# Loading x and the gate weights in the queue of the big transfers

## Chip, cores, metric

The kernel runs on one core of one Trainium2 chip. The metric is the device time of one execution in microseconds (us); lower is better. When a time is given without further words it is a median of several runs.

## The reference, cut to what matters

One token per batch row (B = 2), D = 1024. The model mixes an attention block over a long cache with an MLP block, by a gate.

```python
g = sigmoid((x * gate_w).sum(-1, keepdims=True))        # x: (2, 1, 1024), gate_w: (1024,)
# attention: 32 heads, head size 128, 16384 cached positions, bf16
q = (x @ wq)                                            # wq: (1024, 4096)
p = softmax(einsum("bhqd,bhkd->bhqk", q, k_cache) * 128**-0.5)
a = einsum("bhqk,bhkd->bhqd", p, v_cache)  ... @ wo
b = ...                                                 # layernorm, w1, gelu, w2, layernorm, w3, gelu, w4
return g * a + (1 - g) * b
```

Nearly all the work is reading the K and V caches: 2 x 2 x 32 x 16384 x 128 bf16 values, 537 MB out of the 573 MB that the kernel reads.

## The kernel before

The caches come in 32 steps. A step i needs a K tile and a V tile of 8.39 MB each (two heads of one batch row, 64 KB in each of 128 partitions). Three buffers of that size form a ring (`NBIG = 3`), and wq, which is just as large, goes through the same ring. A transfer is issued, always on SyncE (SP), once the buffer it takes is free: the order is wq, K0, K1 (three buffers, at once), then V0 (takes wq's buffer), K2 (takes K0's), V1 (takes K1's), K3 (takes V0's), and so on.

```python
    def load_rows(keys, srcs):                       # wq, and the MLP weights later
        t = big_tile("wt")
        ...
            nc.sync.dma_start(out=v, in_=src.rearrange("(p r) n -> p r n", p=P))

    x_pm = const.tile([P, B, KC], BF16)              # KC = 8
    gw_pm = const.tile([P, KC], BF16)
    with nc.allow_non_contiguous_dma(reason="a few KB"):
        nc.scalar.dma_start(out=x_pm[:], in_=A_x.rearrange("b s (p r) -> p (b s) r", p=P))
        nc.scalar.dma_start(out=gw_pm[:], in_=gate_w.rearrange("(p r) -> p r", p=P))
    ...                                              # constants
    xT = const.tile([P, KC, B], BF16)
    nc.vector.tensor_copy(out=xT[:], in_=x_pm[:].rearrange("p b r -> p r b"))

    def compute_gate():
        nc.vector.tensor_tensor(out=prod[:], in0=x_pm[:], in1=gw_pm[:]..., op=ALU.mult)
        nc.vector.reduce_sum(out=part[:], in_=prod[:], axis=AX.X)
        ...

    def compute_q():
        wq = wt.pop("wq")
        for h in range(H):
            for r in range(KC):
                nc.tensor.matmul(qps[:, h, :], lhsT=wq[:, r, h * Dh : (h + 1) * Dh], rhs=xT[:, r, :], ...)
        nc.vector.tensor_copy(out=qT[:], in_=qps[:])
        ...                                          # 8 small matmuls, qsel

    def qk_stage(i):                                 # 32 transposes and 64 matmuls on K tile i
        ...
                nc.vector.transpose(out=T[:], in_=Kw[:, m * CJ : (m + 1) * CJ, wh, :])
    ...
    xfers = [("big", "q", lambda: load_rows(["wq"], [A_wq]))]
    steps = [("q", compute_q), ("gate", compute_gate)]
    for i in range(-1, NT):                          # then k{i+1}, v{i}, wo rows, softmax, ...
    ...
    def issue_ready():                               # issue a load when the step that frees its buffer is recorded
```

x_pm takes 16 bytes from each of 2 batch rows for each of 128 partitions: 256 pieces of 16 bytes. gw_pm takes 128 such pieces. A scheduler fixes the order of the instructions on each engine when the program is built. On VectorE it puts `prod` (which needs gw_pm) ahead of `qT`.

## Time and profile before

| | before |
|---|---|
| time, median | 1369.87 us (1369.75 to 1370.2, 3 runs) |
| span of the profiled run | 1367.8 us |
| bytes moved, mean rate | 573.46 MB, 419 GB/s |
| rate from 400 to 800 us | 431 GB/s, DMA share 1.00 |
| rate from 70 to 130 us | 298 GB/s |

The page of the kernel before: its span, the rate in 40 equal slices of 34 us, and the DMA queues (packets, MB, share of 16 engines). q1 is the queue of SP, q10 that of ScalarE (ACT).

```profile
span 1367.8 us, 14339 instructions
...
GB/s 422 434 280 336 428 426 430 434 426 438 426 436 434 434 425 434 428 432 436 435 430 432 434 432 430 432 428 432 430 434 427 431 428 429 432 426 434 431 414 230
...
q1 hardware_dynamic: 15392, 572.53, 97.4%
...
q10 hardware_dynamic: 416, 0.01, 0.0%
```

The stream runs at 414 to 438 GB/s in every slice except the third, the fourth and the last. As the bytes alone take 573.46 / 0.431 = 1330 us at the steady rate, only time in which the DMA engines stand still can be won.

The windows view of the same kernel, by stretch (us from the start): length, then busy time and count for TensorE, its weight load, VectorE, ScalarE and GpSimd, then TensorE's granted clock, the DMA share and GB/s.

```profile
70.00:80.00 10.00, 8.51 (x29) 2.71 (x28) 9.20 (x15) 0.00 (x0) 0.00 (x0) 1.00 0.97 419
80.00:90.00 10.00, 8.34 (x29) 2.60 (x27) 8.76 (x14) 0.00 (x0) 0.00 (x0) 1.00 0.00 1
90.00:100.00 10.00, 5.36 (x18) 2.25 (x18) 7.36 (x16) 0.78 (x2) 0.33 (x1) 0.83 1.03 419
...
110.00:120.00 10.00, 8.97 (x60) 3.51 (x62) 7.63 (x12) 0.00 (x0) 0.34 (x1) 1.00 0.29 105
```

Twice the stream stops (a packet is counted where it starts): from 80 to 90 us, and for some 7 us between 110 and 120 us. VectorE is busy for 88% of the first of these stretches: the core computes, and the DMA engines wait. The timeline of SP (start, length, the issue) shows for what: the next load is issued only when a buffer is free.

```profile
0.74 0.36 SPq L119 DMA_DIRECT2D wt<-in_A_wq_dram  x1
1.16 0.89 SPq L97 DMA_DIRECT2D Kn<-in_A_k_cache_dram  x2
52.20 0.33 SPq L108 DMA_DIRECT2D Vn<-in_A_v_cache_dram  x1
89.54 0.33 SPq L97 DMA_DIRECT2D Kn<-in_A_k_cache_dram  x1
117.49 0.33 SPq L108 DMA_DIRECT2D Vn<-in_A_v_cache_dram  x1
```

K2 is issued at 89.54 us, when K0 has been worked through, and V1 at 117.49 us, when K1 has. Both come after the stream has run dry. The work on K0 itself begins late. From the DMA view (source, queue, size, us from issue to landing) and the timeline of VectorE and TensorE; the bracket is the idle time before, and what ended it:

```profile
x_pm<-in_A_x_dram ACTq DMA_DIRECT2D x1, 4.0 KB, 41.4
wt<-in_A_wq_dram SPq DMA_DIRECT2D x1, 21.9
gw_pm<-in_gate_w_dram ACTq DMA_DIRECT2D x1, 2.0 KB, 61.7
```

```profile
42.12 0.17 DVE L195 COPY xT<-x_pm 128x16 bf16<-128x16 bf16 x1 [39.85 <-DMA x_pm<-in_A_x_dram]
42.35 6.08 PE L237 MATMUL misc<-xT,wt 128*128 128x2 bf16 x223 [42.35 <-DVE xT L195]
...
63.01 0.17 DVE L213 TENSOR_TENSOR prod<-x_pm,gw_pm 128x16 f32<-128x16 bf16 x1 [20.71 <-DMA gw_pm<-in_gate_w_dram]
...
64.36 0.22 DVE L244 CAST qT<-misc 128x64 bf16<-128x64 f32 x1
...
65.93 1.30 DVE L284 STREAM_TRANSPOSE T<-Kn 128x512 f32<-128x512 f32 x2
```

8.39 MB of wq land 21.9 us after issue; 4 KB of x take 41.4 us and 2 KB of gate weights 61.7 us. The projection waits for x until 42 us. Its result qT could be copied at 52 us, but `prod` stands ahead of it on VectorE and waits for the gate weights until 63 us. The first K transpose starts at 65.93 us, long after K0 has landed (42.3 us).

### The profile page before, as it was taken

The page shows a single profiled execution, that of the slowest core. Times are in us where ns is not written, and L with a number is a line of the kernel's source. Part 1 is how long each engine was busy: PE and PEld are TensorE (multiplying, and loading weights), DVE is VectorE, ACT ScalarE, POOL GpSimd, SP SyncE. Part 2 cuts the span into 40 slices and gives each one's busy share as a digit, 9 for nine tenths or more (in the row PEclk, how much of TensorE's full clock was granted, in tenths as well). Part 3 has the DMA queues.
Part 4 walks back from the last instruction along what each step waited for, and adds up shares of the span by engine and source line. Part 5 has one row for each costly group of instructions (what it writes and reads, how often), then busy time and mean ns, then how long its engine had stood idle before and what let it go on. Part 6 is the DMA issues. An engine that isn't in the chain of part 4 may idle for free.

```text
span 1367.8 us, 14339 instructions
## 1 busy us (share of the span) xinstructions
PE 901.4 (66%) x5707; PEld 401.5 (29%) x5770; DVE 783.3 (57%) x1373; ACT 45.0 (3%) x99; POOL 14.3 (1%) x45
## 2 busy tenths in 40 slices
PE   0277766776667766776666676667766666776667
PEld 0223322342223522322222342223222222322224
DVE  0187756755556356666555545566665555666554
ACT  0000000000000000000000000000000000000000
POOL 0000000000000000000000000000000000000000
PEclk9999988868888588888888868888888888888887
DMA  9967999999999999999999999999999999999995
GB/s 422 434 280 336 428 426 430 434 426 438 426 436 434 434 425 434 428 432 436 435 430 432 434 432 430 432 428 432 430 434 427 431 428 429 432 426 434 431 414 230
DMA packets 15876, 573.46 MB, mean 419 GB/s; under 512 B 2369, under 2 KB 2369, under 8 KB 6721
## 3 DMA queue, kind: packets, MB, share of 16 engines
q1 hardware_dynamic: 15392, 572.53, 97.4%
q8 instruction: 45, 0.74, 0.2%
q14 instruction: 23, 0.18, 0.0%
q10 hardware_dynamic: 416, 0.01, 0.0%
HBM read 572.53 MB, written 0.00 MB: 419 GB/s over the span
## 4 chain that ended last, share of the span: by engine, by line
DMA 53%; PE 26%; DVE 16%; another core or an unknown queue 2%; issue 2%; ACT 1%; SPq 0%; ACTq 0%
DMA Kn<-in_A_k_cache_dram 46%; PE S L289 19%; DVE T L284 15%; PE O L333 4%; DMA Vn<-in_A_v_cache_dram 4%; DMA x_pm<-in_A_x_dram 3%; PE misc L343 1%; PE wo_acc L379 1%; ACT Os L341 1%; PE misc L200 1%; ACT Pr L317 0%; DVE PT L321 0%; DVE OT L371 0%; DVE mx L310 0%
## 5 line engine op out<-in xcount | busy, mean ns | idle before, releaser
L284 DVE STREAM_TRANSPOSE T<-Kn 128x512 f32<-128x512 f32 x1024 | 688.3, 701 | 220.6 <-DMA Kn<-in_A_k_cache_dram 152.7
L289 PE MATMUL S<-T,z_135 128*128 128x512 bf16 x992 | 328.4, 419 | 142.9 <-DVE T L284 130.9
L289 PE MATMUL S<-T,z_137 128*128 128x512 bf16 x993 | 325.2, 414 | 144.7 <-DVE T L284 131.8
L289 PEld LDWEIGHTS <-z_135 128*128 128x128 bf16 x1024 | 107.0, 104 | 361.4 <-issue 308.1
L289 PEld LDWEIGHTS <-z_137 128*128 128x128 bf16 x1024 | 106.4, 104 | 360.1 <-issue 305.9
L333 PE MATMUL O<-Vn,PT 128*32 128x512 bf16 x1984 | 114.1, 382 | 0.0
L371 DVE TENSOR_TENSOR OT<-misc,rinv 128x2 bf16<-128x2 f32 x32 | 5.2, 162 | 152.0 <-PE misc L343 144.7
L333 PEld LDWEIGHTS <-PT 128*32 128x32 bf16 x1984 | 70.7, 140 | 43.1 <-issue 13.7
L341 ACT COPY Os<-O 128x512 f32<-128x512 f32 x31 | 18.2, 587 | 1095.4 <-PE O L333 1095.4
L343 PE MATMUL misc<-osel,Os 128*128 128x2 f32 x248 | 32.7, 254 | 12.6 <-ACT Os L341 11.2
L431 PEld LDWEIGHTS <-wt 128*128 128x128 bf16 x576 | 35.9, 169 | 16.4 <-DMA wt<-in_B_w_dram 15.1
L321 DVE STREAM_TRANSPOSE PT<-Pr 128x512 bf16<-128x512 bf16 x32 | 22.7, 711 | 28.7 <-ACT Pr L317 28.7
L237 PE MATMUL misc<-xT,wt 128*128 128x2 bf16 x256 | 7.1, 165 | 45.1 <-DVE xT L195 42.3
L343 PEld LDWEIGHTS misc<-osel,Os 128*128 128x128 f32 x248 | 30.0, 191 | 21.1 <-ACT Os L341 21.1
L300 DVE TENSOR_REDUCE m<-S 128x1 f32<-128x512 f32 x32 | 22.2, 692 | 22.5 <-PE S L289 22.5
L310 DVE TENSOR_REDUCE mx<-misc 64x1 f32<-64x64 f32 x64 | 14.2, 222 | 23.7 <-PE misc L200 23.3
L317 ACT ACTIVATE Pr<-S,nb 128x512 bf16<-128x512 f32 x32 | 22.0, 688 | 122.1 <-DVE nb L312 119.1
L379 PEld LDWEIGHTS <-woh 128*128 128x128 bf16 x256 | 20.7, 168 | 10.4 <-issue 10.2
L195 DVE COPY xT<-x_pm 128x16 bf16<-128x16 bf16 x1 | 0.2, 175 | 39.9 <-DMA x_pm<-in_A_x_dram 39.9
L379 PE MATMUL wo_acc<-OT,woh 128*128 128x2 bf16 x256 | 20.1, 200 | 4.0 <-DVE OT L371 4.0
L200 PE MATMUL misc<-mdiag,ones_f 128*128 128x128 f32 x64 | 16.5, 343 | 8.5 <-DVE mdiag L303 8.5
L237 PEld LDWEIGHTS <-wt 128*128 128x128 bf16 x256 | 7.1, 104 | 45.0 <-DMA wt<-in_A_wq_dram 22.7
(173 smaller groups left out, 160.7 us busy)
## 6 DMA issues: line engine op xcount, KB each, us to landing
wt<-in_B_w_dram SPq DMA_DIRECT2D x2, 7168.0 KB, 46.7
woh<-in_A_wo_dram SPq DMA_DIRECT2D x32, 256.0 KB, 29.9
wt<-in_B_w_dram SPq DMA_DIRECT2D x2, 2048.0 KB, 36.2
Vn<-in_A_v_cache_dram SPq DMA_DIRECT2D x1, 4096.0 KB, 39.5
Vn<-in_A_v_cache_dram SPq DMA_DIRECT2D x1, 2048.0 KB, 43.7
Vn<-in_A_v_cache_dram SPq DMA_DIRECT2D x1, 1024.0 KB, 45.6
Vn<-in_A_v_cache_dram SPq DMA_DIRECT2D x2, 512.0 KB, 47.8
Kn<-in_A_k_cache_dram SPq DMA_DIRECT2D x32, 48.8
```

What stands on the lines that cost most here:

```text
L200: nc.tensor.matmul(ps[:], lhsT=ones_f[:], rhs=src, start=True, stop=True)
L237: nc.tensor.matmul(qps[:, h, :], lhsT=wq[:, r, h * Dh : (h + 1) * Dh], rhs=xT[:, r, :], start=(r == 0), stop=(r == KC - 1),)
L284: nc.vector.transpose(out=T[:], in_=Kw[:, m * CJ : (m + 1) * CJ, wh, :])
L289: nc.tensor.matmul(S[:], lhsT=z[:, 2 * wh + par, NM - 1 - m : NM - 1 - m + P], rhs=Tb[:, :, par], start=(m == 0 and wh == 0 and par == 0), ...
L300: nc.vector.reduce_max(out=m[:], in_=S[:], axis=AX.X)
L317: nc.scalar.activation(out=Pr[:], in_=S[:], func=ACTF.Exp, bias=nb[:], scale=scale, accum_out=rs[:])
L321: nc.vector.transpose(out=PT[:], in_=Pr[:])
L333: nc.tensor.matmul(O[32 * g : 32 * g + 32, :], lhsT=PT[:, m : CJ * 32 : 16], rhs=V[:, j0 : j0 + 4, :], start=(m == 0), stop=(m == NM - 1),)
L341: nc.scalar.copy(out=Os[:].rearrange("p x d -> p (x d)"), in_=O[:])
L343: nc.tensor.matmul(oc[:], lhsT=Os[:, x, :], rhs=osel[:, x, :], start=(x == 0), stop=(x == 3))
L379: nc.tensor.matmul(wo_acc[:, c, :], lhsT=woh[:, :, c], rhs=OT[:, h, :], start=(h == 0 and c == 0), stop=(h == H - 1 and c == KC - 1),)
L431: nc.tensor.matmul(ps[:, c, :], lhsT=w[:, r, :].rearrange("k (p c) -> k p c", c=C)[:, :, c], rhs=actT[:, r, :], start=(r == 0), stop=(r == ...
```

## The change

The intent: x and the gate weights are needed together with wq, so they are put in the same queue right behind wq, ahead of K0. The copy `xT` moves into `compute_q`, as its source is now loaded later in the program. On VectorE the built program then has some constants ahead of `xT` and `prod`; `prod` still stands ahead of `qT`, and the other engines keep their order.

```diff
-    with nc.allow_non_contiguous_dma(reason="a few KB"):
-        nc.scalar.dma_start(out=x_pm[:], in_=A_x.rearrange("b s (p r) -> p (b s) r", p=P))
-        nc.scalar.dma_start(out=gw_pm[:], in_=gate_w.rearrange("(p r) -> p r", p=P))
+
+    def load_first():
+        load_rows(["wq"], [A_wq])
+
+        with nc.allow_non_contiguous_dma(reason="a few KB"):
+            nc.sync.dma_start(out=x_pm[:], in_=A_x.rearrange("b s (p r) -> p (b s) r", p=P))
+            nc.sync.dma_start(out=gw_pm[:], in_=gate_w.rearrange("(p r) -> p r", p=P))
 ... cut ...
     xT = const.tile([P, KC, B], BF16)
-    nc.vector.tensor_copy(out=xT[:], in_=x_pm[:].rearrange("p b r -> p r b"))
 ... cut ...
     def compute_q():
+        nc.vector.tensor_copy(out=xT[:], in_=x_pm[:].rearrange("p b r -> p r b"))
         wq = wt.pop("wq")
 ... cut ...
-    xfers = [("big", "q", lambda: load_rows(["wq"], [A_wq]))]
+    xfers = [("big", "q", load_first)]
```

## The prediction

> **What bounds the kernel.** The DMA stream. The page counts 573.46 MB at a mean 419 GB/s; the windows view shows 431 GB/s and a DMA share of 1.00 from 400 to 1200 us. At 431 GB/s the bytes alone take 1330 us (estimate from these two numbers) of the 1367.8 us span. So a change gains only what it returns to the DMA engines. They fall short in two places: the tail after 1350 us (99, then 11 GB/s), which the change does not touch, and 70 to 130 us: 298 GB/s instead of 431, with whole stretches at nothing (80 to 88 us: 2 and 0 GB/s; 112 to 116 us: 0). That shortfall is 60 x (431-298)/431 = 18.5 us.
>
> **Where the gap comes from.** The timeline: wq has landed by 22.7 us, but x_pm (4 KB, in the ACT queue) lands 41.4 us after its issue and gw_pm (2 KB) 61.7 us after. The query projection starts at 42.3 us; its cast qT stands on VectorE behind prod, which waits for gw_pm until 63.0 us, so the first K transpose starts at 65.9 us, although K0 landed by about 43 us. V0 can be issued at 52.2 us, when the projection has freed wq's buffer, but the next load (K2) needs K0's buffer and is issued only at 89.5 us; V0 had finished by about 80 us. The same happens again at 117.5 us.
>
> Why so late: x needs about 16 pieces of 16 bytes on each of 16 engines plus a completion, and 41.36/17 = 2.43 us is the time one engine needs for a 64 KB row at 431/16 GB/s. This fits the Trainium skill, "DMA: Bandwidth & Descriptors", section "Queues, rings and completion order": an engine goes round-robin between queues at packet granularity. gw: 9 more turns, 20.4 us later. The trace agrees.
>
> **What the change does.** Nothing is removed: the same two transfers stand in the big queue right behind wq, ahead of K0; two issues leave ACT for SP (about 0.5 us each, hidden behind the 22 us of wq). The xT copy (0.175 us) stands later on VectorE; the rest of the order is the same but for constants moved ahead of it. In one ring there are no turns to wait for, so x and gw land about 1 to 2 us behind wq (the output store, the same 4 KB in 16-byte pieces, takes 1.6 us).
>
> Steps after: x and gw land at 23 to 26 us; projection, 7.1 us of matmuls plus the 2.7 us stall seen before, ends at about 34; V0 issued at about 34 (before 52.2); first transpose when K0 lands, about 44 us (before 65.9); K0 done and K2 issued at about 68 (before 89.5), while V0 is in flight until about 83; V1 issued at about 96, K2 in flight until about 102. No gap remains, thereafter the stream is continuous as it already was after 130 us. All compute starts about 22 us earlier, but only the 18.5 us of idle DMA count. The 24 small pieces per engine cost the stream up to about 1 us; they were also paid before.
>
> **Predicted: 1352 us**, 1348 to 1357 (8 in 10); 1.3% less. Faster by over 2%: 0.03; within 2%: 0.96; slower: 0.01.
>
> **Right if:** x_pm to landing falls to about 24 us; first transpose at 43 to 46 us; DMA at 420 or more GB/s in all slices but the last; the tail after the last V unchanged.
>
> **Wrong if:** the small pieces stall the ring they share, delaying K0 by several us (1355 or more); K1's stage frees V1's slot too late (a dip near 100 us stays); or a slower granted clock in the now continuous start takes some back.

## The result and the profile after

| | before | after |
|---|---|---|
| time, median | 1370.01 us (1369.75 to 1370.2, 4 runs) | 1351.17 us (1350.75 to 1351.3, 4 runs) |
| ratio | | 0.9862, 95% interval 0.9845 to 0.9879 |
| span of the profiled run | 1367.8 us | 1349.4 us |
| x_pm, issue to landing | 41.4 us | 21.5 us |
| gw_pm, issue to landing | 61.7 us | 21.3 us |
| first K transpose | 65.93 us | 43.55 us |
| rate from 70 to 130 us | 298 GB/s | 437 GB/s |

A ratio is the mean time of one kernel's runs over that of the other kernel's runs of the same rounds, so it is not quite the ratio of the medians quoted. The gain is 18.8 us, 1.4%: below 2%, but it is far outside the spread of the runs.

The page of the kernel after, the same lines (there is no q10 any more; its 416 packets are in q1):

```profile
span 1349.4 us, 14402 instructions
...
GB/s 405 436 436 434 430 432 428 434 430 428 436 423 436 440 427 424 435 441 428 424 440 434 430 426 436 429 429 440 428 428 440 430 426 419 426 422 438 435 418 220
...
q1 hardware_dynamic: 15808, 572.54, 98.7%
```

The dip in slices three and four is gone; the last slice is as before. The windows view of the kernel after:

```profile
70.00:80.00 10.00, 7.56 (x20) 2.65 (x20) 7.90 (x14) 0.77 (x2) 0.00 (x0) 0.66 0.97 419
80.00:90.00 10.00, 8.67 (x29) 2.79 (x29) 9.99 (x15) 0.00 (x0) 0.00 (x0) 1.00 1.05 454
...
110.00:120.00 10.00, 8.93 (x28) 2.67 (x27) 8.92 (x14) 0.00 (x0) 0.00 (x0) 0.89 1.03 438
```

TensorE's granted clock is lower in places (0.66 from 70 to 80 us, 1.00 before), and it costs nothing here, as the DMA share stays near 1. The timelines of SP and of VectorE after:

```profile
0.74 0.36 SPq L119 DMA_DIRECT2D wt<-in_A_wq_dram  x1
1.16 0.42 SPq L139 DMA_DIRECT2D x_pm<-in_A_x_dram  x1
1.63 0.46 SPq L140 DMA_DIRECT2D gw_pm<-in_gate_w_dram  x1
2.13 1.02 SPq L97 DMA_DIRECT2D Kn<-in_A_k_cache_dram  x2
32.96 0.33 SPq L108 DMA_DIRECT2D Vn<-in_A_v_cache_dram  x1
66.92 0.33 SPq L97 DMA_DIRECT2D Kn<-in_A_k_cache_dram  x1
95.54 0.33 SPq L108 DMA_DIRECT2D Vn<-in_A_v_cache_dram  x1
```

```profile
22.70 0.17 DVE L236 COPY xT<-x_pm 128x16 bf16<-128x16 bf16 x1 [19.45 <-DMA x_pm<-in_A_x_dram]
22.92 0.18 DVE L216 TENSOR_TENSOR prod<-x_pm,gw_pm 128x16 f32<-128x16 bf16 x1
...
43.55 1.30 DVE L288 STREAM_TRANSPOSE T<-Kn 128x512 f32<-128x512 f32 x2 [8.91 <-DMA Kn<-in_A_k_cache_dram]
```

K2 and V1 are issued some 22 us earlier, both while the load ahead of them is still moving, and the first transpose now waits for K0 itself.

Where does the gain come from, and is any of it given back later? The trace records every DMA packet, with its start, length, queue and size. From these one can work out how much later than in the kernel after the big queue of another kernel had moved the same number of bytes. Times are on the clock of the other views, and a packet under way counts in part:

| time in the kernel after, us | 60 | 80 | 90 | 100 | 110 | 200 | 400 | 800 | 1200 | 1330 |
|---|---|---|---|---|---|---|---|---|---|---|
| lag of the kernel before, us | -0.2 | -0.2 | 10.7 | 18.6 | 19.3 | 19.3 | 19.3 | 19.3 | 18.3 | 18.8 |

The whole difference arises in two steps, at the two stops of the stream, 10.9 us and 8.6 us. After 110 us the lag stays between 18.3 and 19.3 us for 1200 us; the two profiled spans differ by 18.4 us, so at most about 1 us is given back. The standstill itself can be counted too: between 80 and 125 us an engine, on average, had no packet of the big queue under way for 18.4 us before and for less than 0.1 us after.

### The profile page after: what moved, and what is told of

The parts are those of the page before. It is cut to its first block, busy times and chain, and to the rows that moved or that the text cites. A ratio compares the mean times of both kernels' runs of the same rounds, so it can differ in the third digit from the quotient of the medians.

```text
span 1349.4 us, 14402 instructions
## 1 busy us (share of the span) xinstructions
PE 918.6 (68%) x5770; PEld 402.5 (30%) x5770; DVE 786.5 (58%) x1373; ACT 45.0 (3%) x99; POOL 14.3 (1%) x45
## 3 DMA queue, kind: packets, MB, share of 16 engines
q1 hardware_dynamic: 15808, 572.54, 98.7%
## 4 chain that ended last, share of the span: by engine, by line
DMA 49%; PE 27%; DVE 18%; issue 2%; another core or an unknown queue 2%; ACT 1%; SPq 0%; ACTq 0%
DMA Kn<-in_A_k_cache_dram 49%; PE S L293 19%; DVE T L288 17%; PE O L337 5%; PE misc L347 1%; PE misc L203 1%; PE wo_acc L383 1%; ACT Os L345 1%; PE misc L354 1%; ACT Pr L321 0%; DVE PT L325 0%; DVE mx L314 0%; DVE OT L375 0%; DVE nb L316 0%
## 5 line engine op out<-in xcount | busy, mean ns | idle before, releaser
L293 PE MATMUL S<-T,z_133 128*128 128x512 bf16 x1024 | 334.3, 420 | 145.0 <-DVE T L288 133.5
L293 PE MATMUL S<-T,z_135 128*128 128x512 bf16 x1024 | 336.3, 423 | 139.4 <-DVE T L288 124.0
L435 PEld LDWEIGHTS <-wt 128*128 128x128 bf16 x576 | 35.8, 172 | 16.0 <-DMA wt<-in_B_w_dram 14.7
L304 DVE TENSOR_REDUCE m<-S 128x1 f32<-128x512 f32 x32 | 22.2, 692 | 22.5 <-PE S L293 22.5
L383 PEld LDWEIGHTS <-woh 128*128 128x128 bf16 x256 | 20.7, 168 | 10.4 <-issue 10.2
L435 PE MATMUL misc<-xn2T,wt 128*128 128x2 bf16 x224 | 14.4, 202 | 7.3 <-DMA wt<-in_B_w_dram 7.3
L435 PE MATMUL misc<-h2T,wt 128*128 128x2 bf16 x224 | 13.6, 199 | 7.0 <-DMA wt<-in_B_w_dram 7.0
```

Source lines behind the costliest of these rows:

```text
L293: nc.tensor.matmul(S[:], lhsT=z[:, 2 * wh + par, NM - 1 - m : NM - 1 - m + P], rhs=Tb[:, :, par], start=(m == 0 and wh == 0 and par == 0), ...
L304: nc.vector.reduce_max(out=m[:], in_=S[:], axis=AX.X)
L383: nc.tensor.matmul(wo_acc[:, c, :], lhsT=woh[:, :, c], rhs=OT[:, h, :], start=(h == 0 and c == 0), stop=(h == H - 1 and c == KC - 1),)
L435: nc.tensor.matmul(ps[:, c, :], lhsT=w[:, r, :].rearrange("k (p c) -> k p c", c=C)[:, :, c], rhs=actT[:, r, :], start=(r == 0), stop=(r == ...
```

## The experiments

Two questions are open after the comparison. First: why did 4 KB need 41 us? My theory was that the DMA engines alternate between the two queues, one small piece against one 64 KB row. Rivals: 16-byte pieces, or this queue, are slow in themselves. Second: how does a late start turn into lost time? My theory was that only an issue that comes after the stream has run dry costs anything. The rival: the time follows the first K transpose one for one.

In all experiments the result was correct. Moving the `xT` copy alone was not run: the program that is built has the same order of instructions on all engines as the kernel before. `x_own_gw_behind_k0` and `gw_18_turns` came last, after the others were known.

### wq in four pieces (`wq_quarters`)

The kernel before, with its queues as they are, but shorter rows in the big queue while x and gw load.

```diff
-            nc.sync.dma_start(out=v, in_=src.rearrange("(p r) n -> p r n", p=P))
+            sv = src.rearrange("(p r) n -> p r n", p=P)
+            step = 2 if key == "wq" else R
+            for r0 in range(0, R, step):
+                nc.sync.dma_start(out=v[:, r0 : r0 + step, :], in_=sv[:, r0 : r0 + step, :])
```

> The kernel before, x and gw still in the ACT queue, but wq is loaded in four pieces, so one row in the big queue is 16 KB instead of 64 KB. Theory (one small piece per turn, and a turn lasts as long as one row of the big queue): a turn is a quarter of 2.43 us, 0.61 us, so x_pm lands about 17 x 0.61 = 10.5 us and gw_pm about 26 x 0.61 = 16 us after issue (before 41.4 and 61.7), both ahead of wq; first K transpose at 43 to 44 us and the time that of the changed kernel, 1351 us. Rival (16-byte pieces, or this queue, are slow in themselves): x_pm and gw_pm stay at 41 and 62 us, 1370 us.

Measured: 1351.09 us (4 runs), ratio to before 0.9862 (0.9847 to 0.9876). The DMA view:

```profile
x_pm<-in_A_x_dram ACTq DMA_DIRECT2D x1, 4.0 KB, 12.7
gw_pm<-in_gate_w_dram ACTq DMA_DIRECT2D x1, 2.0 KB, 17.2
```

In the packet records a row of 64 KB took 2.418 us on its engine and a row of 16 KB 0.611 us. The small loads became 3.3 and 3.6 times faster although nothing about them was changed, neither their pieces nor their queue. So neither is slow in itself: the length of the rows in the other queue sets their pace. The whole gain comes without moving them, and with the order of instructions on the compute engines as before, so the changed order on VectorE is not what brings it. The landings are 1 to 2 us later than expected; the first small packet starts 2.7 us after the issue of x, which I had not counted.

### One of the two small loads put back (`gw_own_queue`, `x_own_queue`, `half_x`)

All three start from the kernel after and put part of the small loads back into the ACT queue.

```diff
 # gw_own_queue
+        nc.scalar.dma_start(out=gw_pm[:], in_=gate_w.rearrange("(p r) -> p r", p=P))
     def load_first():
         load_rows(["wq"], [A_wq])
             nc.sync.dma_start(out=x_pm[:], in_=...)
-            nc.sync.dma_start(out=gw_pm[:], in_=gate_w.rearrange("(p r) -> p r", p=P))
 # x_own_queue: the same with x_pm instead of gw_pm
 # half_x: ACT queue: x_pm[:, 0:1, :] from A_x[0:1], then gw_pm; behind wq: x_pm[:, 1:2, :] from A_x[1:2]
```

> The changed kernel with gw put back into the ACT queue, x stays behind wq. Theory (turns): gw_pm needs 9 turns only, with no x ahead of it, and lands 9 x 2.43 = 22 us after issue, as early as wq; no loss, 1351 us. Rival (a small load in a queue of its own is late by itself, by some 40 us or more): gw_pm still at 40 to 62 us; by 62 us the first transpose would be back at 65 us and the time near 1370 us.

> The changed kernel with x put back into the ACT queue, gw stays behind wq. Theory: x_pm lands at about 42 us as before, projection 42 to 52 us, V0 issued at 52 us, first transpose at 54 us (before 65.9, after 43.6). K2 would be issued at 77 us, before V0 ends (82), but V1 only at 106 us, about 5 us after K2 has ended at about 101: one gap of 5 us plus some 1.5 us of restart, 1357 us (1355 to 1359). Rival A (only x matters): 1370 us. Rival B (time follows the first transpose one for one): 1351.2 + 10.4 = 1361.6 us.

> The changed kernel with half of x (one of the two batch rows, 128 pieces) and then gw put back into the ACT queue; the other half of x stays behind wq. Theory: half of x lands after 9 turns, 22 us, so the projection is not late; gw after 18 turns, 43 to 44 us, so the first transpose starts at 46 to 47 us, 3 us later than after the change. That lies within the slack (V1 issued at about 98.5 us, K2 ends at about 101): no gap, 1351.2 us. Rival (time follows the first transpose one for one): 1354.3 us.

Measured: 1350.96, 1351.04 and 1351.11 us (4 runs each), ratios 0.9861 (0.9845 to 0.9878), 0.9861 (0.9847 to 0.9876) and 0.9861 (0.9846 to 0.9876). The first came as expected: gw_pm landed 22.2 us after issue. The other two did not. x_pm should have landed at 42 us in `x_own_queue`:

```profile
x_pm<-in_A_x_dram ACTq DMA_DIRECT2D x1, 4.0 KB, 22.3
wt<-in_A_wq_dram SPq DMA_DIRECT2D x1, 22.1
gw_pm<-in_gate_w_dram SPq DMA_DIRECT2D x1, 2.0 KB, 22.0
```

and gw_pm of `half_x` landed at 22.3 us instead of 43. Either the turns were wrong, or I had counted them wrongly. The packet records decide it. They show for each packet of the ACT queue when it started; there are 16 engines, so 16 packets are one for each engine.

| ACT queue, packets started | in all | during wq | in the 2 us at wq's end | during K0 | in the 2.5 us at K0's end | later |
|---|---|---|---|---|---|---|
| before (x, then gw) | 416 | 112 | 32 | 112 | 32 | 128 |
| x_own_queue (x) | 272 | 112 | 160 | 0 | 0 | 0 |
| half_x (half of x, then gw) | 288 | 112 | 176 | 0 | 0 | 0 |

During wq all three moved 7 packets per engine, one for each 64 KB row: the alternation is there. The difference is at wq's end. In `x_own_queue` the big queue then holds the 8 pieces of gw per engine and its completion, packets of 16 and 4 bytes that take 0.009 us each. Against these a turn costs nothing, and the last 10 packets per engine of x went through within 1 us. In the kernel before, K0 came next and only 2 packets per engine went through at that point. So the count of turns was right and their cost was not: a turn costs what the other queue's next packet takes, and I had placed small packets there.

### x in its own queue, gw behind K0 (`x_own_gw_behind_k0`)

This is the test of that explanation: the same queue for x, but no small packets at wq's end. It starts from the kernel after. Its expectation was written with the result of `gw_first` (below) known: that is the second of the "two slow points".

```diff
+        nc.scalar.dma_start(out=x_pm[:], in_=A_x.rearrange("b s (p r) -> p (b s) r", p=P))
     def load_first():
         load_rows(["wq"], [A_wq])
 ...
     def load_k(i):
         ...
         kn_tiles[i] = t
+        if i == 0:
+            load_gw()          # nc.sync, gw_pm
```

The scheduler now puts `qT` ahead of `prod` and `prod` between the first transposes; apart from that, and from the place of two small matmuls on TensorE and of two small operations on VectorE that go with them, the order on the engines is that of before.

> In x_own_queue x landed at 22 us, not at 42. Its packets show why: its 17 packets per engine had 8 turns against 64 KB rows of wq, the rest against the small packets of gw, which stood behind wq in the big queue and cost nothing. So here the same queue for x, but gw stands behind K0 in the big queue: at the end of wq there are no cheap turns. Theory: x_pm lands at 41 to 42 us again, projection 42 to 52 us (49 if the 2.9 us stall is missing), first K transpose at 54 us (51). V1 is then issued at about 105.5 us (102.5). From the two slow points measured (first transpose at 65.9: +18.8 us; at 70.7: +23.4 us) the loss is about the first transpose minus 47.2: 7 us (4 us if no stall), 1358 us (1354 to 1360). Rival A (no ACT-queue load is late unless it has another one behind it): x_pm at 22 us, 1351 us. Rival B (time follows the first transpose one for one): 1351.2 + 10.4 = 1361.6 us (1358.7).

Measured: 1359.83 us (1358.97 to 1360.48, 6 runs), ratio to before 0.9925 (0.9912 to 0.9939). x_pm landed 41.4 us after issue, to the tenth as in the kernel before. Of its packets 112 started during wq, 32 at its end, 112 during K0. The first rival (a load in that queue is late only if another one stands behind it there) falls. The first transpose started at 53.13 us, V1 was issued at 106.78 us, and the windows view shows one stop of the stream instead of two:

```profile
80.00:90.00 10.00, 6.68 (x17) 2.36 (x18) 7.02 (x14) 0.78 (x2) 0.00 (x0) 0.66 1.08 465
90.00:100.00 10.00, 8.68 (x30) 2.73 (x29) 10.00 (x15) 0.00 (x0) 0.00 (x0) 1.00 0.87 375
100.00:110.00 10.00, 9.05 (x72) 3.75 (x74) 7.45 (x11) 0.00 (x0) 0.33 (x1) 1.00 0.32 105
110.00:120.00 10.00, 5.34 (x38) 2.89 (x31) 4.24 (x12) 1.36 (x3) 0.00 (x0) 0.80 0.97 419
```

K2 came in time, V1 did not. The time is at the upper edge of what was expected. This run also shares out the gain: with x late but gw out of the way the loss against the kernel after is 8.7 us, so the late gw behind it adds the other 10.2 of the 18.8 us. (Taken in the other order the shares would differ, as there is a slack; see the end of this section.)

### The two small loads swapped (`gw_first`)

```diff
-        nc.scalar.dma_start(out=x_pm[:], in_=A_x.rearrange("b s (p r) -> p (b s) r", p=P))
         nc.scalar.dma_start(out=gw_pm[:], in_=gate_w.rearrange("(p r) -> p r", p=P))
+        nc.scalar.dma_start(out=x_pm[:], in_=A_x.rearrange("b s (p r) -> p (b s) r", p=P))
```

> The kernel before with the two small loads swapped in the ACT queue: gw first, x second. No work is added. Theory: gw_pm lands after 9 turns, about 22 us; x_pm after all 26 turns, at 62 to 63 us (41.4 us to landing before); the projection runs from 63 to 73 us, V0 is issued at 73 us with the stream empty since K1 ended at 63, the first transpose starts at 75 us, V1 is issued at about 127 us against 101.5 without gaps: 1378 us (1375 to 1381), slower than before. Rival (the sum of both loads is what counts, the order does not): 1370 us.

Measured: 1374.52 us (4 runs), ratio to before 1.0033 (1.0016 to 1.005): the interval lies above 1, so a little slower, though no work was added. gw_pm landed 22.1 us after issue, x_pm after 60.7 us. The order counts, because the projection needs only x. The time was 3.5 us less than expected and just below the range given, because the first transpose started at 70.72 us instead of 75: the projection started at 62.13 us instead of 63, and it ran through here (256 matmuls in 6.97 us), while near its end it stands still for 2.7 us before and 2.9 us after.

### Ahead of wq (`ahead`), and in the queue of GpSimd (`pool_queue`)

```diff
 # ahead (from the kernel after)
     def load_first():
-        load_rows(["wq"], [A_wq])
         ... x_pm and gw_pm on nc.sync ...
+        load_rows(["wq"], [A_wq])
 # pool_queue (from the kernel before)
-        nc.scalar.dma_start(out=x_pm[:], ...)      # and gw_pm
+        nc.gpsimd.dma_start(out=x_pm[:], ...)      # and gw_pm
```

> The changed kernel with x and gw in the big queue ahead of wq instead of behind it. Theory: they land 2 to 3 us after issue; wq and everything behind it moves by at most 1 us; nothing waited for x or gw at the end of wq, so the time is that of the changed kernel, 1351 us, within 1 us. Rival (the 24 small pieces per engine hold up a large queue while nothing else is in it): wq lands several us later and the time grows by as much, 1354 us or more.

> The kernel before with x and gw issued from GpSimd instead of ACT, so again a queue of their own, but descriptors made by software. If each 16-byte piece takes a turn of its own here too: x_pm at about 42 us, gw_pm at about 62 us, 1370 us: any queue beside the big one is late. If software bundles many pieces into one packet, x needs a few turns only: x_pm and gw_pm within 3 to 15 us, 1351 us: then what counts is the number of packets, not the queue.

Measured: `ahead` 1351.85 us, ratio 0.9867 (0.9853 to 0.9882); x_pm and gw_pm land 1.8 and 1.9 us after issue, and the big stream lags 0.7 to 0.8 us behind that of the kernel after from 40 to 800 us: here the first row of wq starts at 2.76 us instead of 1.73. Behind wq the same packets cost nothing that could be measured (K1 landed at about 63 us both before and after). `pool_queue` 1351.56 us, ratio 0.9864 (0.985 to 0.9879), and it lands early from a queue of its own:

```profile
x_pm<-in_A_x_dram POOLq DMA_DIRECT2D x1, 4.0 KB, 9.5
gw_pm<-in_gate_w_dram POOLq DMA_DIRECT2D x1, 2.0 KB, 14.0
```

The packet records show why: in this queue x is one packet of 256 bytes per engine, plus one of 4 bytes, where the ACT queue had 16 of 16 bytes plus one. Two turns instead of 17. So it is not the separate queue that makes a small load late, but the number of its packets times the time of the other queue's packets.

### gw needing 18 turns (`gw_18_turns`)

This one asks how late the first transpose may be without a loss.

```diff
 # from the kernel before
+    gw_twin = const.tile([P, KC], BF16)            # loaded, never used
-        nc.scalar.dma_start(out=x_pm[:], ...)
+        nc.gpsimd.dma_start(out=x_pm[:], ...)
+        nc.scalar.dma_start(out=gw_twin[:], in_=gate_w.rearrange("(p r) -> p r", p=P))
         nc.scalar.dma_start(out=gw_pm[:], in_=gate_w.rearrange("(p r) -> p r", p=P))
```

> The kernel before, x moved to the GpSimd queue (it landed at 10 us there), and in the ACT queue gw loaded twice, first into an unused tile, so that the gw which is used needs 18 turns. Theory: gw_pm lands at 43 to 44 us; the projection is on time (V0 issued at 33 to 34 us); first transpose at 46 to 47 us instead of 43.6 to 44.3. That is inside the slack: V1 is issued at about 98.5 us, before K2 has ended at about 101. No gap, 1351.2 to 1351.9 us. Rival (time follows the first transpose one for one): 1354 us or more.

Measured: 1353.85 us (1352.39 to 1354.64, 4 runs), ratio to before 0.988 (0.9866 to 0.9895). gw_pm landed 43.0 us after issue and the first transpose started at 47.14 us, as expected, but there was a loss of 2.7 us where I had expected none. I had compared the issue of V1 (99.09 us) with the end of K2 (its last rows end at 99.7 to 101.6 us, by engine) and forgotten that the first packets of a load start later than its issue: for K2 in the kernel before, issued at 89.54 us to an idle stream, at 90.49 us on the first engine and 91.20 us on the last, so 0.95 to 1.7 us later. V1's first row here starts at 100.05 us, when some engines were already idle. The profiled run took 2.4 us more than that of the kernel after. Its stream lags 0.4 us from before the stop on, 1.4 us at 110 us and 2.0 us from 260 us on. So about 1.0 us arises at V1. The 0.7 us that come between 240 and 260 us, and the rest, I cannot explain.

Taken together, the kernels give the loss as a function of when V1 is issued:

| kernel | first K transpose | V1 issued | time | loss against after |
|---|---|---|---|---|
| after | 43.55 | 95.54 | 1351.17 | 0 |
| pool_queue | 44.29 | 96.04 | 1351.56 | 0.4 |
| gw_18_turns | 47.14 | 99.09 | 1353.85 | 2.7 |
| x_own_gw_behind_k0 | 53.13 | 106.78 | 1359.83 | 8.7 |
| before | 65.93 | 117.49 | 1370.01 | 18.8 |
| gw_first | 70.72 | 122.40 | 1374.52 | 23.4 |

(The kernel before measured 1370.01 to 1370.08 us.) For the two latest the loss is the issue of V1 minus 98.7 and minus 99.0 us, for the two in between minus 96.4 and minus 98.1. The rival, one for one with the first transpose, would give 22.4 us for before and 27.2 us for gw_first: 3.5 and 3.8 us more than measured. It falls there. For gw_18_turns it gives 3.6 us against 2.7 measured, and for x_own_gw_behind_k0 9.6 against 8.7, which alone would not decide it. The 0.4 us of pool_queue are within the spread of the runs. There is a slack, and the packet records of the kernel after give an estimate of its size: the engines finish the rows of K2 at 99.4 to 101.2 us, and a load issued by 98.4 us could have its first packet there, 0.95 us later, when the first engine is through; V1 is issued at 95.54, so the slack is some 3 us, not the 6 us that the prediction's numbers imply. That gw_18_turns loses more than the 0.7 us that this estimate allows it stays open.

## Why the prediction was right

- **The DMA stream is the bound, and only its idle time counts.** Right. All compute started 22.4 us earlier, and 18.8 us were won. 18.5 us had been read off the rate from 70 to 130 us. The lag table shows the two stops, and that at most about 1 us is given back later.
- **The small loads are late because of turns at packet granularity.** Right, and shown by `wq_quarters`, `x_own_gw_behind_k0` and the packet records: 7 small packets per engine during wq, one per 64 KB row. This is as the Trainium skill says in "DMA: Bandwidth & Descriptors", section "Queues, rings and completion order". The arithmetic 41.36/17 = 2.43 us was partly luck: the first small packet starts only some 5 us into the run, and turns against completions of the big queue are free (2 packets per engine at wq's end instead of 1). The two roughly cancel. Where I used the same count in the experiments without looking at what the other queue holds next, it failed (`x_own_queue`, `half_x`).
- **They land 1 to 2 us behind wq.** Slightly better: xT could be copied at 22.70 us, and wq had landed by 22.5 us. The cost to the stream, predicted as at most about 1 us, was not measurable behind wq and 0.7 us ahead of it.
- **The steps after.** V0 issued at 34 (measured 32.96), first transpose at 44 (43.55), K2 issued at 68 (66.92), V1 at 96 (95.54). The projection's 2.7 us stall appeared again (2.89). The time from the landing of the last V to the end stayed at 5.2 us, as predicted. One of the conditions that it set for being right was missed by a little: 420 GB/s or more in all slices but the last. The page has 405 in the first slice and 419 and 418 in two late ones; before, the first had 422 and the last but one 414.
- **V1's slack.** The step was right in its sign; its size was generous: 102 - 96 = 6 us in the prediction, some 3 us by the table above. The terms mis-sized are the time between an issue and its first packet, left out (0.95 us on the first engine), and the end of K2: the first engine ends its rows at 99.4 us, not 102. It did no harm, because the change stays on the right side of it.
- **The granted clock.** It was lower from 70 to 130 us (0.86 against 0.93), and took nothing back.

## What to carry to other kernels

A small load with many short pieces should not stand alone in a queue beside one with long rows if something waits for it: each of its packets may wait for a whole row of the other queue. Put it into the big queue right behind (or, for a little, ahead of) the transfer it is needed with; shorter rows in the big queue while it loads, or fewer and larger packets, did as well here. And in a kernel bound by its loads, a late start costs what it makes the stream stand still, so look at when the buffers come free, not at the idle time of the compute engines.

## What the Trainium skill lacked or had wrong

- "DMA: Bandwidth & Descriptors", section "Queues, rings and completion order", gives 9 to 17 descriptors as a typical packet. In the ACT queue here each 16-byte piece was a packet of its own (416 packets for 384 pieces and 32 completions), and in the SP queue each 64 KB row (2.418 us). From GpSimd, 16 pieces were one packet of 256 bytes, which fits the page. It lacks the consequence: a small load's delay is the number of its packets times the other queue's packet time (41.4 us for 4 KB, 12.7 us with 16 KB rows, 9.5 us in packets of 256 bytes).
- The same page, section "Issuing engines are not separate DMA queues", says that issuing from several engines only saves the time to initiate. It lacks that it can cost: 18.8 us of 1370 us here, by two small loads.
- The same page, "Latency and other measured facts", gives about 600 ns to the first byte for this kind of queue. The number fits if it is counted from the end of the issuing instruction: K2 of the kernel before was issued from 89.54 to 89.87 us, and its first packet started at 90.49 us, 0.62 us later. The page lacks that the 16 engines do not start together: the last of them started at 91.20 us.
- No page that I read says what stops TensorE for 2.7 to 2.9 us in the projection under full DMA load. "Runtime: NRT & Kernel Launch", section "Instruction fetch mechanics", tells of instruction fetches in 16 KiB blocks, but not that they could wait for other DMA traffic. A 16 KB packet of the instruction queue started at 29.5 us, inside the stall of the kernel after (29.0 to 31.9 us). In `gw_first` such packets started at 64.9 and 68.4 us, inside the projection too, but with the big stream empty, and there was no stall; it is the only one of the 11 kernels without it. That an instruction fetch waits for turns like x and gw is what this suggests; no run was made to show it.
